# One more chunk of the first layer by seven products, and the weight sums held behind the splits

## The chip, the cores and the metric

The kernel runs on one core of a Trainium2 chip. The metric is the device time of one execution in microseconds, the median of the runs shown.

## What is computed

Pooled attention (keys and values averaged over 8 tokens, so 576 tokens see 72 pooled ones), and after it a two-layer network with a leaky ReLU, all of it in float32.

```python
B, H, S, D = 8, 8, 576, 64            # q is 8x, k is 8x the drawn values
k_p = k.reshape(B, H, 72, 8, D).mean(axis=3)
v_p = v.reshape(B, H, 72, 8, D).mean(axis=3)
scores = matmul(q, k_p.T) / 8;  attn = softmax(scores)
x = matmul(attn, v_p)                  # as 4608 rows of 512
h = x @ w_in                           # 512 -> 2048
out = maximum(0.01 * h, h) @ w_out     # 2048 -> 512
```

## The kernel before

**Chunks and runs.** The 4608 rows are worked as nine chunks of 512, numbered 0 to 8 (chunk 6 is the seventh). The network is most of the work. A float32 operand is split into a high and a low part (types fp32r), and a product of two such operands is three matmuls: high by high, high by low, low by high. The first layer of a chunk is 16 steps `f` of 128 hidden units; one step (`m1`, L1141 to L1143) is 12 matmuls of 512 columns into the PSUM tile `ph`. ScalarE (ACT) then applies the leaky ReLU in place (L1146) and makes the high part `gh` (L1149), VectorE (DVE) makes the low part `gl` (L1150). The second layer of a step (`m2`, L1327 to L1329) is again 12 matmuls of 512 columns, into four accumulators, and it trails `m1` by two steps. `ph` has two buffers, so `m1` of step f+2 can start only when `gl` of step f is done. `runs` lists the chunks in order: the first five entries share out chunks 0 and 1, after that each entry is one chunk, 2 to 8.

**Attention beside it.** The attention that fills chunk c+1 is done during the run of chunk c. TensorE (PE) makes the scores `pss` (L599), ACT the exponentials (L609), GpSimd (POOL) the normalized rows `at` (L643, L649). These go to DRAM and come back turned (`rows`, `blocks`, issued by SyncE, SP), DVE turns them (L680), ACT and DVE split them into `pT` (L702, L705), and PE multiplies by the pooled values (`pa`, L724 to L727). ACT and DVE write the result as the split tiles `xh`, `xl` of the next chunk.

**Keys and values.** `lk` and `lv` load and pool the keys and values of one batch: SP issues the loads of `k0raw`, `k1raw`, `kremraw`, `v0raw`, `v1raw`, `vremraw`, POOL adds them up (L264, L271) to `ksum`, `vsum`, `vremsum`. ACT scales `ksum` (L349), and later, when the batch's turn comes, `v_hi` (L512) and `v_parts` (L521) are made of the value sums. The raw tiles all come from the pool tag `raw`, which has two buffers.

**Seven products.** From chunk `FAST` on, the first layer goes by pairs of steps: a 2 by 2 block product in seven block products in place of eight (`pair`, `product`, L1233), each six matmuls of 256 columns, 42 to a pair, eight pairs to a chunk. It needs sums of weight blocks. `prepare(j)` makes them for pair j (DVE L1180 to L1186, ACT `wsumh` L1189, DVE L1190), in two tiles of the tag `raw`, and SP writes them to the DRAM tile `kept` (L1200). They come back for each pair through ACT's queue (`stream`, L1225). `combine` makes sums and splits of the x blocks (POOL L797, ACT, DVE L793). The eight pairs' weight sums are spread over four runs, chunks 2 to 5, two pairs each, in the first half of each run; `lk` and `lv` stand at the middle of a run's attention units.

**What sets the order.** PE's order is written out by hand. The other engines' orders are made by a scheduler, which fills each queue with what its own model of the time finds ready, so that an instruction can stand ahead of others that the program issued before it. From the first seven-product chunk on (`pinned`), POOL's and SP's orders are the program's too, and attention follows `line_up_pinned` in place of `line_up_via`. `tc.issue_after(ins)` holds back what is issued inside it until `ins` is in its queue. An engine works its queue strictly in order.

Of the kernel before, what the change touches and what calls it, by code (L numbers as in the profile page):

```python
# [24 lines left out]
def tile_pooled_attention_ffn(  # L25
# [44 lines left out]
    VIA = 2  # L70
    SPLIT = 8
    HALF = CH // 2
    FAST = 7


    PAIRS = [(4, 0), (5, 1), (6, 2), (7, 3), (8, 9), (10, 11), (12, 13), (14, 15)]
# [422 lines left out]
    def place_v(b, sums, rem):  # L499
        if b < 2:  # L500
            pvm = bank(b, f"pvm{b}").rearrange("a p x -> a (p x)")[:, : NK * D]
            for g, half in enumerate(sums):
                for i in range(2):
                    nc.tensor.matmul(
                        pvm[:, 2 * g * D : 2 * (g + 1) * D],
                        addup[:, 1 - i : 3 - i, :].rearrange("r i s -> r (i s)"),
                        half[:, i::2, :], start=i == 0, stop=i == 1,
                    )
            sums = pvm.rearrange("a (p d) -> a p d", p=NK)
        for i in range(2):  # L510
            r = slice(64 * i, 64 * i + 64)
            pin(nc.scalar.mul(v_hi[r, :, i, :], sums[r], 1.0 / POOL))  # L512
        for i in range(2):
            r = slice(64 * i, 64 * i + 64)
            pin(nc.vector.scalar_tensor_tensor(
                v_lo[r, :, i, :], sums[r], 1.0 / POOL, v_hi[r, :, i, :].bitcast(F32),
                op0=ALU.mult, op1=ALU.subtract,
            ))
        if b > 1:
            yield  # L520
            pin(nc.scalar.mul(v_parts, rem, 1.0 / POOL))  # L521
            yield
            pin(nc.vector.scalar_tensor_tensor(
                rem, rem, 1.0 / POOL, v_parts.bitcast(F32), op0=ALU.mult, op1=ALU.subtract
            ))
            nc.vector.tensor_scalar(rem, rem, signs[:, 1:2], None, op0=ALU.mult)
            nc.vector.scalar_tensor_tensor(
                rem, v_parts.bitcast(F32), signs[:, 0:1], rem, op0=ALU.mult, op1=ALU.add
            )
            nc.vector.tensor_tensor(  # L530
                v_rem, rem.unsqueeze(2).broadcast_to([P, 2, 4, D]),
                heads.unsqueeze(1).unsqueeze(3).broadcast_to([P, 2, 4, D]), op=ALU.mult,
            )
            return
        for g in range(2):
            r, lo = slice(32 * g, 32 * g + 32), slice(64 + 32 * g, 96 + 32 * g)
            nc.scalar.mul(v_parts[r, g], rem[r, 0], 1.0 / POOL)
            nc.vector.scalar_tensor_tensor(
                v_parts[lo, g], rem[r, 0], 1.0 / POOL, v_parts[r, g].bitcast(F32),
                op0=ALU.mult, op1=ALU.subtract,  # L540
            )
        pv = bank(b, f"pv{b}").rearrange("a p x -> a (p x)")[:, : 2 * D]
        nc.tensor.matmul(
            pv, spread, v_parts.rearrange("s g d -> s (g d)"), start=True, stop=True
        )
        nc.vector.tensor_tensor(
            v_rem, pv.rearrange("s (g d) -> s g d", g=2).unsqueeze(2).broadcast_to([P, 2, 4, D]),
            heads.unsqueeze(1).unsqueeze(3).broadcast_to([P, 2, 4, D]), op=ALU.mult,
        )
# [574 lines left out]
    parts = [(n, c, f) for n, (c, fs, _) in enumerate(runs) for f in fs]  # L1124
    partial = dram.tile([CH, DM], F32, name="partial")
    back = []
    gs, accs = {}, {}

    def m1(k):

        n, c, f = parts[k]
        xh, xl = x_parts(c)
        w = ws[0, f]
        ts = runs[n][2]
        r = slice(ts[0] * P, (ts[-1] + 1) * P)
        w_ = len(ts) * P
        nm = f"{n}_{f}"
        ph = ps_h.tile([P, CH], F32, tag="h", name=f"ph{nm}")[:, :w_]
        for kk in range(NK):
            ks = slice(kk * P, (kk + 1) * P)  # L1140
            nc.tensor.matmul(ph, w[:, 0, ks], xh[kk][:, r], start=kk == 0, stop=False)  # L1141
            nc.tensor.matmul(ph, w[:, 0, ks], xl[kk][:, r], start=False, stop=False)  # L1142
            nc.tensor.matmul(ph, w[:, 1, ks], xh[kk][:, r], start=False, stop=kk == NK - 1)  # L1143
            if kk == 1:
                yield
        nc.scalar.activation(ph, ph, AF.Prelu, alpha=0.01)  # L1146
        gh = three.tile([P, CH], F32R, tag="gh", name=f"gh{nm}")[:, :w_]
        gl = three.tile([P, CH], F32R, tag="gl", name=f"gl{nm}")[:, :w_]
        casts.append(nc.scalar.copy(gh, ph))  # L1149
        nc.vector.tensor_tensor(gl, ph, gh.bitcast(F32), op=ALU.subtract)  # L1150
        gs[k] = gh, gl
        yield

# [16 lines left out]
    def prepare(j):  # L1170

        f0, f1 = PAIRS[j]
        raw = two.tile([P, 2, DM], F32, tag="raw", name=f"wsum{j}")
        w = [raw[:, k, :] for k in range(2)]
        raw = two.tile([P, 2, DM], F32R, tag="raw", name=f"wsumh{j}")
        h = [raw[:, k, :] for k in range(2)]
        (a11, a12), (a21, a22) = ((x[:, :HALF], x[:, HALF:]) for x in w)
        for x, f in zip(w, (f0, f1)):
            whole = ws[0, f].bitcast(F32)
            nc.vector.tensor_tensor(x, whole[:, 0, :], whole[:, 1, :], op=ALU.add)  # L1180
            yield
        nc.vector.tensor_tensor(a22, a21, a22, op=ALU.add)
        nc.vector.tensor_tensor(a21, a11, a21, op=ALU.subtract)
        yield
        nc.vector.tensor_tensor(a11, a22, a11, op=ALU.subtract)
        nc.vector.tensor_tensor(a12, a12, a11, op=ALU.subtract)  # L1186
        yield
        for x, y in zip(w, h):
            nc.scalar.copy(y, x)  # L1189
            nc.vector.tensor_tensor(x.bitcast(F32R), x, y.bitcast(F32), op=ALU.subtract)  # L1190
            yield
        ship = [
            (kept[j, :, 2 - 2 * i : 4 - 2 * i, k, :], part.rearrange("p (s x) -> p s x", s=2))
            for i in range(2) for k, part in enumerate((h[i].bitcast(F32), w[i]))
        ]
        if j < OPEN:
            ship.append((kept[j, :, 4], ws[0, f1].bitcast(F32)[:, :, HALF:]))
        yield
        for to, of in ship:
            nc.sync.dma_start(to, of)  # L1200
        yield

    seats = {}
# [139 lines left out]
    def store(n, c, t, a):  # L1343
        end = n == len(runs) - 1
        if end and t == NT - 1:

            r = 2 * S - 2 * TAIL + (c - 2) * CH + t * P
            for i, copy in enumerate((nc.scalar.copy, nc.vector.tensor_copy)):
                cols = slice(i * DM // 2, (i + 1) * DM // 2)
                o = two.tile([P, DM // 2], F32, tag="raw", name=f"o{n}_{t}{i}")  # L1350
                copy(o, a[:, cols])
                (nc.scalar if i == 0 else nc.sync).dma_start(out[r : r + P, cols], o)
            return

        pool, tag = (two, "raw") if n == REST - 1 and t > 1 else (five, "o")
        o = pool.tile([P, DM], F32, tag=tag, name=f"o{n}_{t}")
        if end:
            if t % 2:
                nc.scalar.copy(o, a)
            else:  # L1360
                nc.vector.tensor_copy(o, a)
        elif n == REST:
            nc.vector.tensor_tensor(o, a, back[t], op=ALU.add)
        else:
            nc.scalar.copy(o[:, : DM // 2], a[:, : DM // 2])
            nc.vector.tensor_copy(o[:, DM // 2 :], a[:, DM // 2 :])
        if n == 0:
            nc.sync.dma_start(partial[t * P : (t + 1) * P, :], o)
        elif c < 2:
            nc.sync.dma_start(out[c * S + t * P : c * S + (t + 1) * P, :], o)  # L1370
        elif c == 2 and t == 0:
            for b in range(2):
                nc.sync.dma_start(out[b * S + CH : (b + 1) * S, :], o[TAIL * b : TAIL * (b + 1), :])
        else:
            r = 2 * S - 2 * TAIL + (c - 2) * CH + t * P
            nc.sync.dma_start(out[r : r + P, :], o)


    steps = []
# [99 lines left out]
        early[max(n, REST) - 1].append(b)  # L1479

    PIECES_OF = 8
    EACH = -(-len(PAIRS) // (FAST - 3))

    def sums_of(js):
        for j in js:
# [4 lines left out]
    for n, (c, fs, ts) in enumerate(runs[: REST + FAST - 1]):  # L1490
# [3 lines left out]
        if n >= REST:  # L1494
            nxt = n - REST + 2
            if nxt in waiting:
                us.insert(0, lambda nxt=nxt: carry(nxt))
            mid = len(us) // 2
            for b in early[n]:
                us[mid:mid] = [att[b]["lk"], att[b]["lv"]]  # L1500
            if n == REST:
# [5 lines left out]
        for f in fs:  # L1507
# [23 lines left out]
            for slot in slots:  # L1531
                for _ in slot:
                    beat += 1
                    while done < min(len(us), len(us) * beat // (beats - behind)):
                        us[done]()
                        done += 1
                    while n > REST and formed < min(1, 2 * beat / beats) * PIECES_OF * EACH:
                        formed += 1
                        next(forming, None)
            at += 1  # L1540
        while done < len(us):
            us[done]()
# [80 lines left out]
```

## Time and profile before

| | |
|---|---|
| median of 3 runs | 923.64 us (922.68, 923.64, 926.41) |
| profiled execution | 926.44 us, span 924.7 us |
| PE busy, share of span | 890.6 us, 96% |
| DVE, ACT, POOL busy | 499.3, 433.4, 211.2 us |
| granted TensorE clock, mean | 0.987 |
| chunk 2's run | 253.0 to 355.6 us |
| chunk 3's run | 355.6 to 450.5 us |
| chunk 4's run | 450.5 to 548.8 us |
| chunk 5's run | 548.8 to 645.3 us |
| chunk 6's run | 645.3 to 739.2 us |
| chunk 7's run (seven products) | 739.2 to 830.5 us |
| chunk 8's run (seven products, no attention beside it) | 830.5 us to the end |

A run is taken from the start of its chunk's first first-layer matmul to that of the next chunk's. PE's busy share counts pipelined matmuls and says little about how dense they are; the distance between the starts of two matmuls in the timeline does.

### The profile page before, as it was taken

The numbers are of one execution on the slowest core, as the hardware profiler recorded it, in microseconds if no ns is written. First come the engines' busy times: TensorE is split into PE (matmuls) and PEld (weight loads), VectorE is DVE, ScalarE is ACT, GpSimd is POOL, SyncE is SP. The second block draws the span as 40 slices with busy tenths as digits, with TensorE's granted clock in tenths as the row PEclk, the third lists the DMA queues.
The fourth block names the chain that finished last, engine by engine and source line by source line (L and its number), as shares of the span: only waits on it lengthen the run. The fifth ranks groups of instructions, "written<-read, shape, count | busy, mean of one in ns | idle before, by whom it ended". The sixth has DMA issues, their size and how long they took to land.

```text
span 924.7 us, 13658 instructions
## 1 busy us (share of the span) xinstructions
PE 890.6 (96%) x4587; PEld 761.1 (82%) x4587; DVE 499.3 (54%) x1178; ACT 433.4 (47%) x1354; POOL 211.2 (23%) x388
## 2 busy tenths in 40 slices
PE   4599999999999989999999999999999999999998
PEld 4478888788888868888888878888888889989997
DVE  6999569545384572636555555553455442452222
ACT  5788558344344443533444345342544344453332
POOL 4511110343423312411232122411210321010000
PEclk9799999999999989999999999999999999999999
DMA  9985231427346453423534343620532055414342
GB/s 259 303 262 166 66 72 46 97 58 188 111 130 171 107 162 86 113 47 120 154 82 96 87 137 102 138 62 25 148 81 63 0 164 160 122 47 137 105 135 80
DMA packets 153029, 108.37 MB, mean 117 GB/s; under 512 B 99840, under 2 KB 133376, under 8 KB 152960
## 3 DMA queue, kind: packets, MB, share of 16 engines
q1 hardware_dynamic: 144976, 90.86, 36.4%
q10 hardware_dynamic: 7984, 16.65, 6.4%
q8 instruction: 36, 0.59, 0.3%
q14 instruction: 33, 0.27, 0.1%
HBM read 76.94 MB, written 30.54 MB: 116 GB/s over the span
## 4 chain that ended last, share of the span: by engine, by line
PE 80%; DVE 7%; DMA 5%; POOL 2%; SPq 2%; ACT 2%; issue 1%; POOLq 0%; ACTq 0%; DVEq 0%
PE acc L1327 12%; PE acc L1328 12%; PE acc L1329 12%; PE ph L1141 9%; PE ph L1143 9%; PE ph L1142 9%; PE ends_y L1233 5%; PE ends_x L1233 3%; PE pss L599 3%; DMA q<-in_q_dram 1%; DMA blocks<-rows 1%; PE pa L725 1%; PE pa L727 1%; PE pa L726 1%; PE pa L724 1%
## 5 line engine op out<-in xcount | busy, mean ns | idle before, releaser
L1327 PE MATMUL acc<-w,gh 128*128 128x512 f32 x576 | 227.6, 395 | 0.0
L1328 PE MATMUL acc<-w,gh 128*128 128x512 f32 x576 | 225.2, 391 | 0.0
L1329 PE MATMUL acc<-w,gl 128*128 128x512 f32 x576 | 224.5, 390 | 0.0
L1141 PE MATMUL ph<-xh,w 128*128 128x512 f32 (+1 forms) x480 | 185.4, 386 | 3.6 <-DVE gl L1150 3.6
L1142 PE MATMUL ph<-xl,w 128*128 128x512 f32 (+1 forms) x480 | 181.9, 379 | 0.0
L1143 PE MATMUL ph<-xh,w 128*128 128x512 f32 (+1 forms) x480 | 181.9, 379 | 0.0
L1329 PEld LDWEIGHTS acc<-w,gl 128*128 128x128 f32 x576 | 108.2, 188 | 23.4
L1146 ACT ACTIVATE ph<-ph 128x512 f32<-128x512 f32 (+1 forms) x120 | 67.1, 559 | 127.0 <-PE ph L1143 126.3
L609 ACT ACTIVATE e<-pss,red 128x72 f32<-128x72 f32 (+1 forms) x320 | 97.6, 328 | 57.5 <-DVE red L607 57.2
L1327 PEld LDWEIGHTS acc<-w,gh 128*128 128x128 f32 x576 | 108.5, 188 | 19.2
L1328 PEld LDWEIGHTS acc<-w,gh 128*128 128x128 f32 x576 | 108.5, 188 | 18.6
L1150 DVE TENSOR_TENSOR gl<-ph,gh 128x512 fp32r<-128x512 f32 (+1 forms) x120 | 77.6, 648 | 74.7 <-ACT gh L1149 73.7
L1141 PEld LDWEIGHTS ph<-xh,w 128*128 128x128 f32 x480 | 91.5, 191 | 19.8 <-DVE gl L1150 4.2
L1143 PEld LDWEIGHTS ph<-xh,w 128*128 128x128 f32 x480 | 91.3, 190 | 16.9
L1142 PEld LDWEIGHTS ph<-xl,w 128*128 128x128 f32 x480 | 91.4, 190 | 15.4
L643 POOL TENSOR_TENSOR at<-e,red 128x128 f32<-128x128 f32 (+1 forms) x120 | 48.4, 423 | 193.1 <-DVE red L640 116.1
L1149 ACT CAST gh<-ph 128x512 fp32r<-128x512 f32 (+1 forms) x120 | 67.1, 559 | 3.1
L609 ACT ACTIVATION_READ_ACCUMULATOR e<-pss,red 128x1 f32 (+1 forms) x320 | 68.4, 214 | 0.0
L607 DVE TENSOR_REDUCE red<-pss 128x4 f32<-128x288 f32 (+1 forms) x80 | 35.9, 453 | 55.8 <-PE pss L599 53.1
L680 DVE STREAM_TRANSPOSE pp<-blocks 128x384 f32<-128x384 f32 (+1 forms) x60 | 44.4, 760 | 38.6 <-DMA blocks<-rows 38.5
L702 ACT CAST pT_hi<-pp 128x384 fp32r<-128x384 f32 (+1 forms) x80 | 36.4, 479 | 45.9 <-DVE pp L680 42.6
L599 PE MATMUL pss<-kT,qT 128*128 128x144 f32 x320 | 48.8, 294 | 3.8 <-DVE qT L564 1.1
(244 smaller groups left out, 1263.5 us busy)
## 6 DMA issues: line engine op xcount, KB each, us to landing
seat<-kept ACTq DMA_DIRECT2D x21, 512.0 KB
rows<-at SPq DMA_DIRECT2D x48, 192.0 KB
blocks<-rows SPq DMA_DIRECT2D x48, 192.0 KB
out_dram<-o SPq DMA_DIRECT2D x34, 256.0 KB
w_bits<-in_moe_w_in_dram SPq DMA_DIRECT2D x16, 512.0 KB
w_bits<-in_moe_w_out_dram SPq DMA_DIRECT2D x16, 512.0 KB
q<-in_q_dram SPq DMA_DIRECT2D x96, 64.0 KB
kept<-wsumh SPq DMA_DIRECT2D x16, 256.0 KB
```

The costliest lines, as they stand in the source:

```text
L599: nc.tensor.matmul(sc[:, 2 * SP * i : 2 * SP * (i + 1)], qT[:, p, :], kT[:, p, :, :].rearrange("d i s -> d (i s)"), start=True, stop=True,)
L609: ins = nc.scalar.activation(e[:n, h, :], scv[:n, h, :], AF.Exp, bias=mx[:n, h : h + 1], accum_out=sm[:n, h : h + 1],)
L1141: nc.tensor.matmul(ph, w[:, 0, ks], xh[kk][:, r], start=kk == 0, stop=False)
L1142: nc.tensor.matmul(ph, w[:, 0, ks], xl[kk][:, r], start=False, stop=False)
L1143: nc.tensor.matmul(ph, w[:, 1, ks], xh[kk][:, r], start=False, stop=kk == NK - 1)
L1146: nc.scalar.activation(ph, ph, AF.Prelu, alpha=0.01)
L1149: casts.append(nc.scalar.copy(gh, ph))
L1150: nc.vector.tensor_tensor(gl, ph, gh.bitcast(F32), op=ALU.subtract)
L1233: nc.tensor.matmul(out, w[:, stay, ks], move, start=start and i + n == 0, stop=i + n == 3, skip_group_check=True,)
L1327: nc.tensor.matmul(a, gh[:, r], hi, start=first, stop=False)
L1328: nc.tensor.matmul(a, gh[:, r], lo, start=False, stop=False)
L1329: nc.tensor.matmul(a, gl[:, r], hi, start=False, stop=last)
```

## The change

Chunk 6 is now worked with seven products, with all that hangs on it (its attention results go unsplit to `x_next`, its attention beside follows the pinned order, POOL and SP are pinned one run earlier). The weight sums still stand in four runs, chunks 2 to 5, two pairs each, but from beat 8 to beat 30 of a run's 64 (a beat is half an `m1` or half an `m2`), and each piece is held back until the last `gh` and `gl` issued so far are in their queues. `lk` and `lv` stand at two thirds of a run's attention units. `v_parts` is held back behind `v_hi`. The copy of a resident weight half to `kept` is held back behind the last store of the output.

```diff
-    FAST = 7
+    FAST = 6
...
-            pin(nc.scalar.mul(v_hi[r, :, i, :], sums[r], 1.0 / POOL))
+            ins = pin(nc.scalar.mul(v_hi[r, :, i, :], sums[r], 1.0 / POOL))
...
-            pin(nc.scalar.mul(v_parts, rem, 1.0 / POOL))
+            with tc.issue_after(ins.ins):
+                pin(nc.scalar.mul(v_parts, rem, 1.0 / POOL))
...
-        nc.vector.tensor_tensor(gl, ph, gh.bitcast(F32), op=ALU.subtract)
+        lows.append(nc.vector.tensor_tensor(gl, ph, gh.bitcast(F32), op=ALU.subtract))
...
-        if j < OPEN:
-            ship.append((kept[j, :, 4], ws[0, f1].bitcast(F32)[:, :, HALF:]))
         yield
         for to, of in ship:
             nc.sync.dma_start(to, of)
+        if j < OPEN:
+            with tc.issue_after(sent[-1].ins):
+                nc.sync.dma_start(kept[j, :, 4], ws[0, f1].bitcast(F32)[:, :, HALF:])
...
-            nc.sync.dma_start(out[r : r + P, :], o)
+            sent.append(nc.sync.dma_start(out[r : r + P, :], o))
...
-    EACH = -(-len(PAIRS) // (FAST - 3))
+    EACH = -(-len(PAIRS) // (FAST - 2))
+    FROM, UNTIL = 8, 30
...
-            mid = len(us) // 2
+            mid = len(us) * 2 // 3 if n > REST else len(us) // 2
             for b in early[n]:
                 us[mid:mid] = [att[b]["lk"], att[b]["lv"]]
...
-                    while n > REST and formed < min(1, 2 * beat / beats) * PIECES_OF * EACH:
+                    while n > REST and formed < min(1, (beat - FROM) / (UNTIL - FROM)) * PIECES_OF * EACH:
                         formed += 1
-                        next(forming, None)
+                        with tc.issue_after(casts[-1].ins), tc.issue_after(lows[-1].ins):
+                            next(forming, None)
```

In the rows below a name's first digits are its batch, tile or step: `ph5_11` is step 11 of chunk 2 (the sixth entry of `runs`, counted from 0), `ph6_9` step 9 of chunk 3, `wsumh2` the high part for the third pair, `o9_0` the first output tile of chunk 6, `o8_0` that of chunk 5.

ACT's queue in the second half of chunk 2's run, before:

```order
L609 ACTIVATE e3_2_0_3469,red3_2_0_3470<-pss3_2_0_3466,red3_2_0_3470 64x72 x4
L609 ACTIVATE e3_2_1_3479,red3_2_1_3480<-pss3_2_1_3476,red3_2_1_3480 64x72 x4
L1189 CAST wsumh2_3741<-wsum2_3740 128x512 x2
L521 ACTIVATE v_parts_107<-vremsum4_3296 128x128
L1146 ACTIVATE ph5_11_3506<-ph5_11_3506 128x512
L702 CAST pT_hi_118<-pp3_0_0_3553 128x3x128
L1149 CAST gh5_11_3520<-ph5_11_3506 128x512
```

and in the changed kernel:

```order
L610 ACTIVATE e3_2_0_3469,red3_2_0_3470<-pss3_2_0_3466,red3_2_0_3470 64x72 x4
L610 ACTIVATE e3_2_1_3479,red3_2_1_3480<-pss3_2_1_3476,red3_2_1_3480 64x72 x4
L1147 ACTIVATE ph5_11_3506<-ph5_11_3506 128x512
L703 CAST pT_hi_118<-pp3_0_0_3553 128x3x128
L1150 CAST gh5_11_3520<-ph5_11_3506 128x512
```

The third pair's `wsumh` and the next batch's `v_parts` stood ahead of step 11's ReLU; now neither does. The third pair's casts now stand in chunk 3's run, behind `gh6_3`, and that batch's `v_parts` behind its `v_hi`.

ACT's queue where `ksum` of batch 5 is scaled, in chunk 3's run, before:

```order
L1146 ACTIVATE ph6_3_3927<-ph6_3_3927 128x512
L349 ACTIVATE ksum5_4170<-ksum5_4170 128x256
L1149 CAST gh6_3_3948<-ph6_3_3927 128x512
L1146 ACTIVATE ph6_4_3977<-ph6_4_3977 128x512
L1149 CAST gh6_4_4002<-ph6_4_3977 128x512
```

and in the changed kernel:

```order
L703 CAST pT_hi_118<-pp3_4_1_4244 128x3x128
L1147 ACTIVATE ph6_8_4217<-ph6_8_4217 128x512
L1150 CAST gh6_8_4238<-ph6_8_4217 128x512
L349 ACTIVATE ksum5_4313<-ksum5_4313 128x256
L610 ACTIVATE e4_1_0_4264,red4_1_0_4265<-pss4_1_0_4261,red4_1_0_4265 128x72 x4
L610 ACTIVATE e4_1_1_4274,red4_1_1_4275<-pss4_1_1_4271,red4_1_1_4275 128x72 x4
L1147 ACTIVATE ph6_9_4281<-ph6_9_4281 128x512
L1150 CAST gh6_9_4303<-ph6_9_4281 128x512
```

The scaling moved from step 3 to behind step 8, nine rows and two steps behind the last `wsumh` of the run (not shown), whose buffers the key loads take over; two groups of exponentials and step 9's ReLU stand behind it.

DVE's queue at the start of the first seven-product run, before (chunk 7):

```order
L1366 COPY o9_0_7558<-acc9_0_6725 128x256
L1366 COPY o9_1_7565<-acc9_1_6729 128x256
L1264 TENSOR_TENSOR gl10_0_7546<-dia10_0_7468,gh10_0_7545 128x512
L1366 COPY o9_2_7595<-acc9_2_6741 128x256
L1264 TENSOR_TENSOR gl10_0_7589<-off10_0_7467,gh10_0_7588 128x512
L1366 COPY o9_3_7604<-acc9_3_6745 128x256
L564 STREAM_TRANSPOSE qT7_3_7624<-q7_3_6936 128x4x128
```

and in the changed kernel (chunk 6):

```order
L1369 COPY o8_0_6677<-acc8_0_5763 128x256
L565 STREAM_TRANSPOSE qT6_3_6681<-q6_3_5986 128x4x128
L1266 TENSOR_TENSOR gl9_0_6669<-dia9_0_6580,gh9_0_6668 128x512
L1369 COPY o8_1_6686<-acc8_1_5767 128x256
L608 TENSOR_REDUCE red6_3_0_6718<-pss6_3_0_6714 128x4
L608 TENSOR_REDUCE red6_3_1_6728<-pss6_3_1_6724 128x4
L1266 TENSOR_TENSOR gl9_0_6711<-off9_0_6579,gh9_0_6710 128x512
L640 TENSOR_TENSOR red6_3_0_6718<-red6_3_0_6718,tiny_120 128x4
L641 RECIPROCAL red6_3_0_6718<-red6_3_0_6718 128x4
L565 STREAM_TRANSPOSE qT6_4_6787<-q6_4_6654 128x2x4x32
L1369 COPY o8_2_6737<-acc8_2_5781 128x256
```

The turned queries of the second attention tile stood behind all four output copies and stand now behind one; those of the third stand ahead of the third and fourth.

## Rows read from the trace of the kernel before

**Rows 1.** The page: busy time of each engine, and the chain that ended last by engine.
```profile
PE 890.6 (96%) x4587; PEld 761.1 (82%) x4587; DVE 499.3 (54%) x1178; ACT 433.4 (47%) x1354; POOL 211.2 (23%) x388
...
PE 80%; DVE 7%; DMA 5%; POOL 2%; SPq 2%; ACT 2%; issue 1%; POOLq 0%; ACTq 0%; DVEq 0%
```

**Rows 2.** Stretches, chunks 2 to 8: length, busy (count) by engine, clock, DMA share, GB/s.
```profile
253.00:355.60 102.60, 99.39 (x458) 83.14 (x458) 62.94 (x151) 43.31 (x143) 31.90 (x55) 0.97 0.51 136
355.60:450.50 94.90, 94.90 (x449) 79.80 (x448) 50.27 (x118) 38.85 (x124) 20.08 (x40) 1.00 0.38 101
450.50:548.80 98.30, 96.72 (x457) 81.27 (x456) 55.89 (x139) 43.00 (x146) 26.40 (x51) 1.00 0.41 107
548.80:645.30 96.50, 96.50 (x458) 81.28 (x457) 47.45 (x119) 40.00 (x138) 26.27 (x51) 1.00 0.35 86
645.30:739.20 93.90, 93.90 (x447) 79.15 (x445) 46.85 (x113) 43.12 (x143) 19.27 (x39) 1.00 0.27 72
739.20:830.50 91.30, 90.22 (x569) 81.49 (x568) 38.98 (x81) 42.23 (x125) 13.37 (x23) 1.00 0.43 125
```

**Rows 3.** Timeline of PE, chunk 2's run: start, length, what, idle before and its releaser.
```profile
331.36 0.79 PE L1141 MATMUL ph<-xh,w 128*128 128x512 f32 x1 [3.21 <-DVE gl L1150]
```

**Rows 4.** Timeline of ACT, the same place.
```profile
327.51 1.14 ACT L1189 CAST wsumh<-wsum 128x512 fp32r<-128x512 f32 x2 [7.34 <-POOL vremsum L271]
328.56 0.30 ACT L521 ACTIVATE v_parts<-vremsum 128x128 fp32r<-128x128 f32 x1
328.77 0.57 ACT L1146 ACTIVATE ph<-ph 128x512 f32<-128x512 f32 x1
```

**Rows 5.** Stretch behind that stall: columns as in rows 2.
```profile
331.00:337.00 6.00, 5.64 (x14) 4.49 (x15) 5.28 (x13) 1.83 (x4) 0.00 (x0) 0.50 0.79 254
```

**Rows 6.** Timeline, chunk 4's run: ACT, then PE.
```profile
533.26 1.15 ACT L1189 CAST wsumh<-wsum 128x512 fp32r<-128x512 f32 x2 [8.64 <-POOL vremsum L271]
...
539.68 0.39 PE L725 MATMUL pa<-pT_lo,v_hi 128*128 128x256 f32 x1 [1.58 <-DVE pT_lo L705]
```

**Rows 7.** Timeline of PE, one `m1` of 12 matmuls: its first, and what follows its last.
```profile
322.55 0.39 PE L1141 MATMUL ph<-xh,w 128*128 128x512 f32 x1
...
325.26 0.39 PE L1327 MATMUL acc<-w,gh 128*128 128x512 f32 x1
```

**Rows 8.** Chain in order of time: two block products (12 matmuls) of chunk 7.
```profile
739.36 1.43 PE ends_x L1233 x12
```

**Rows 9.** Groups by line, chunk 7: weight loads of a block product, count | busy, mean ns.
```profile
L1233 PEld LDWEIGHTS ends_x<-T17xh,seat 128*128 128x128 f32 x32 | 5.6, 192 | 0.0
```

**Rows 10.** Timeline, chunk 7's run: ACT, DVE, PE around its one stall.
```profile
754.35 0.37 ACT L1365 COPY o<-acc 128x256 f32<-128x256 f32 x1 [1.33 <-DMA out_dram<-o]
...
754.76 0.42 DVE L1366 COPY o<-acc 128x256 f32<-128x256 f32 x1 [2.85 <-ACT o L1365]
755.10 1.07 DVE L564 STREAM_TRANSPOSE qT<-q 128x512 f32<-128x512 f32 x1
...
756.23 1.00 PE L599 MATMUL pss<-kT,qT 128*128 128x144 f32 x6 [1.08 <-DVE qT L564]
```

**Rows 11.** Groups by line and shape: ReLU, high part, low part of a step.
```profile
L1146 ACT ACTIVATE ph<-ph 128x512 f32<-128x512 f32 x104 | 61.0, 587 | 122.6 <-PE ph L1143 121.9
...
L1149 ACT CAST gh<-ph 128x512 fp32r<-128x512 f32 x104 | 61.1, 588 | 2.7
...
L1150 DVE TENSOR_TENSOR gl<-ph,gh 128x512 fp32r<-128x512 f32 x104 | 70.9, 683 | 71.4 <-ACT gh L1149 70.5
```

**Rows 12.** Timeline, chunk 2's run: key loads on SP, `ksum` on ACT.
```profile
288.02 1.32 SPq L287 DMA_DIRECT2D k0raw<-in_k_dram  x2
...
298.27 0.42 ACT L349 ACTIVATE ksum<-ksum 128x256 f32<-128x256 f32 x1 [6.10 <-POOL ksum L271]
298.59 0.58 ACT L1146 ACTIVATE ph<-ph 128x512 f32<-128x512 f32 x1
```

**Rows 13.** Timeline of POOL, end of chunk 6's run: the last x sum of `combine`.
```profile
728.61 1.74 POOL L797 TENSOR_TENSOR x<-x,x 128x512 f32<-128x512 f32 x1
```

More of the change, by code (lines that the diff above doesn't have):

```diff
@@ L1126, in tile_pooled_attention_ffn @@
     back = []
-    gs, accs = {}, {}
+    gs, accs, lows, sent = {}, {}, [], []
     def m1(k):
@@ L1353, in store @@
             return
-        pool, tag = (two, "raw") if n == REST - 1 and t > 1 else (five, "o")
+        apart = n == REST - 1 and t > 1
+        pool, tag = (two, "raw") if apart else (five, "o")
         o = pool.tile([P, DM], F32, tag=tag, name=f"o{n}_{t}")
@@ L1369, in store @@
         elif c < 2:
-            nc.sync.dma_start(out[c * S + t * P : c * S + (t + 1) * P, :], o)
+            sent.append(nc.sync.dma_start(out[c * S + t * P : c * S + (t + 1) * P, :], o))
         elif c == 2 and t == 0:
```

## The prediction

> **What bounds the kernel.** I read the page first, then the stretches chunk by chunk, then PE's timeline wherever a stretch is longer than its work, and last what released the engine that PE waited for. The page names PE: it is busy for 96% of the span, and 80% of the chain that ended last is PE [rows 1]. So time is won in two ways only, by giving PE less to stream or by closing holes in its stream. The stretches show where the holes are: chunks 3, 5 and 6 have PE busy from end to end, chunk 2 lacks 3.2 us, chunk 4 1.6 us and chunk 7 1.1 us [rows 2]. Chunks 2 and 5 have the same 458 matmuls in them, yet chunk 2 takes 102.6 us and chunk 5 96.5.
>
> **The hole in chunk 2.** PE idles 3.21 us before an `m1` and is released by `gl` [rows 3]. `gl` is late because ACT stood still for 7.34 us, until POOL's `vremsum` let go of the buffer into which the cast `wsumh` writes [rows 4]; the ReLU of the step came only after it, at 328.77. That cast belongs to the third pair, whose sums the program issues in chunk 3's run; the scheduler had drawn it forward. Behind the hole the granted clock is 0.50, the 1.2 GHz level, from 331 to 337 us with PE busy [rows 5]; before it PE had run at 2.4 GHz without a gap. So chunk 2's excess over chunk 5 is the idle time, 3.2 us, and some 2.9 us of half clock. Chunk 4 has the same cast, waiting 8.64 us for the same releaser, and PE then idles 1.58 us for `pT` [rows 6]; the clock stays up.
>
> **The change, part by part.**
>
> *Sums behind the splits, `v_parts` behind `v_hi`, key loads later.* ACT's queue shows both waiting instructions gone from ahead of step 11's ReLU, and the third pair's casts back in chunk 3, between two steps. Their buffers come there from value loads of the run before, long pooled. The work is the same, 16 casts and their DVE steps, only moved, and it stays beside PE's stream. I take the two holes as gone whole: 102.6 - 96.5 = **-6.1 us** for chunk 2 and 98.3 - 96.5 = **-1.8 us** for chunk 4 [rows 2]. Bounds: nothing, if another wait takes their place, and these sums, since chunk 5 has no hole to give.
>
> *Seven products in chunk 6.* Removed are 16 `m1`. One is 325.26 - 322.55 = 2.71 us from first start to the next matmul behind it [rows 7], so 16 are 43.4 us. Added are 8 pairs of 7 block products; two of these take 1.43 us [rows 8], so 56 take 40.0 us. The difference is **-3.3 us**. The second layer and the attention's matmuls stay as they are. The trace bounds it well, because chunk 7 already runs this way.
>
> What speaks against a finer cut is the weight load: 336 loads of 128 columns in place of 192. A load of a block product lasts 192 ns [rows 9], yet twelve matmuls with their twelve loads pass in 1.43 us [rows 8], so the loads lie under the matmuls before them. The Trainium skill, in "TensorE: Matmul & The Clock Gate", Part 3 (what overlaps and what doesn't), says that a weight load overlaps with matmuls in flight only where it goes to other row groups, and these go to all rows; by that the 144 more loads would stand in PE's way, and the sum would be that of the last rival below. The trace does not agree.
>
> *What the seven products bring with them, at no cost on PE.* Weight sums come back through ACT's queue for chunk 6 too: chunk 7 has a DMA share of 0.43 against chunk 6's 0.27 [rows 2], so both loads together come to no more than 0.70, under the 0.79 that the trace shows for a short while [rows 5]. `combine` now ends chunk 5, where attention, key loads and weight sums also lie. Its last POOL step ended at 730.4 us, 8.9 us before the 739.2 at which chunk 7 began [rows 13]. In the new order POOL has the next batch's value sums just ahead of it; if these come 9 us later than before, the start of chunk 6 waits. In rows 2 POOL is busy 26 of 96 us in chunk 5, so I take zero.
>
> *The start of the pinned run.* Chunk 7's one hole is at its start: an output tile waits for a store, DVE's copy waits for ACT's, the turned queries stand behind it, and PE waits 1.08 us for the scores' operand [rows 10]. The same start now comes at chunk 6 and again at chunk 7. The new queue has the second tile's queries behind one output copy in place of four, which speaks for less; five attention tiles beside chunk 6 in place of three speak for more. I price chunk 6's start as the row has it, **+1.1 us**, and leave chunk 7's as it was. Bounds: -1.1 (both gone) and +3.
>
> *The key scaling.* The loads now begin only when the run's second pair of sums has been written out, and the scaling of `ksum` on ACT stands two or three steps behind that pair's last cast, with exponentials and a ReLU queued behind it. From the first key load to the scaling took 298.27 - 288.02 = 10.3 us [rows 12]; two steps of `m1` and `m2` are 4 x 2.71 = 10.8 us. So ACT comes to the scaling at about the moment it can go, or a few us early, since the sums must first land. The slack is: `gl` of a step is wanted when two `m2` and one `m1` have passed, 3 x 2.71 = 8.1 us, less ReLU, `gh` and `gl`, 0.59 + 0.59 + 0.68 [rows 11], which leaves 6.3 us. A wait of 6.10 us on this very scaling cost PE nothing [rows 12], one of 7.34 us cost 3.2 [rows 4]. I take zero; the bounds are 0 and 6.1 us a chunk (3.2 idle and 2.9 of half clock, as in chunk 2).
>
> **The sum.** -6.1 - 1.8 - 3.3 + 1.1 = -10.1 us, against the profiled execution's own 926.44 us (924.7 of span and 1.7 around it): **916.3 us**. That execution is 2.8 us above the median of 923.64; two of the runs shown lie near 923 and one near 926.4. The gap is about what the half clock cost, but no row tells whether the others had it, and a kernel without the hole has neither, so I forecast from the profiled one. Against the median it is -7.3 us, 0.8%. A measurement of this kernel can tell about 0.5% from no change, 4.6 us: faster is under 919.0, slower over 928.3.
>
> **The rivals.**
>
> 1. *The wait comes back at the key scaling, in one of the four runs* (chunks 2 to 5). For it: key loads moved behind the sums, and 4 us of exponentials queue behind the scaling. Against it: 6.10 us cost nothing. 916.3 + 6.1 = 922.4 us. Chance 0.14.
> 2. *The same in three or four of the runs*, since all four have the same order. It decides where ACT's wait passes some 6 us of slack on every run, that is where the key loads land 4 to 6 us later than I reckon. Four times 6.1: 916.3 + 24.4 = 940.7 us, slower than before. Chance 0.06.
> 3. *Attention beside the pinned chunk 6 holds PE up.* Five tiles in place of three, with POOL's and SP's order fixed, or `combine` late at the end of chunk 5. At chunk 7's hole for each tile, five times 1.1, in place of one: 916.3 + 4.4 = 920.7 us. For it: the order was followed with three tiles only. Against it: DVE, ACT and POOL are under half busy there [rows 2]. Chance 0.10.
> 4. *The holes stay*: the cast is held at the tail of another wait and chunks 2 and 4 lose what they lost. 916.3 + 7.9 = 924.2 us. Against it the queue's order, plainly. Chance 0.04.
> 5. *Weight loads stand in the way*: 144 more loads at 192 ns [rows 9] are 27.6 us in place of the 3.3 won: 947 us. Chunk 7's 91.3 us, with 336 such matmuls, rules it out. Chance 0.01.
>
> That leaves 0.65 for the forecast: holes gone, seven products at their streamed cost, a stray hole of a microsecond or two.
>
> **How the numbers follow.** The likeliest case gives 916.3. Its own range is 912.5 (both pinned starts clean, and small gaps closed) to 919.0. To hold 8 in 10 the range must reach rival 3 and the first chunk of rival 1: 912.5 to 922.5; left out are rivals 2, 4 and 5 and the far side of 1. Faster by over 0.5%: 0.65 for the forecast, less 0.03 for its upper edge, and 0.13 from the milder half of rivals 1 and 3 (a hole without half clock, 3.2 us, ends near 919), 0.75. Slower: rivals 2 and 5, 0.07. Within: the rest, 0.18.
>
> **What would show it.** Right: chunk 2 at 96 to 97 us and chunk 4 at 96.5 with PE busy throughout; no wait of `wsumh` or `v_parts` for `vremsum`; the clock at 1.00 from chunk 2 to the end; chunk 5 about 2.7 us shorter than before and chunk 6 near 94.4, because four second-layer tiles pass from the one to the other, 12 matmuls at 0.226 us (chunk 6's stretch has 447 matmuls where its neighbours have up to 458 [rows 2]). Wrong: ACT waiting over 6 us for `ksum` with PE idle for `gl` behind it (rivals 1 and 2); holes before the scores or `pT` in chunk 6 (rival 3); 56 block products over 42 us (rival 5).

## The result, and the profile after

| | before | after |
|---|---|---|
| median | 924.44 us (922.68 to 926.41, 4 runs) | 938.40 us (937.79 to 939.08, 4 runs) |
| ratio, 95% interval | | 1.0150 (1.0132 to 1.0168) |
| profiled execution, span | 926.44, 924.7 us | 938.04, 936.2 us |
| mean granted clock | 0.987 | 0.984 |

The change costs 1.5%. The lengths of chunks here and below are each of one profiled execution, and executions of one kernel differ by 1 to 5 us; the medians and their intervals decide. The stretches of the kernel after, chunks 2 to 7, with the columns of [rows 2]:

```profile
253.00:357.00 104.00, 98.95 (x458) 82.39 (x457) 55.55 (x131) 40.29 (x138) 28.50 (x51) 0.98 0.42 109
357.00:459.50 102.50, 97.70 (x450) 81.45 (x449) 49.74 (x118) 38.85 (x124) 25.60 (x44) 0.97 0.38 103
459.50:555.90 96.40, 96.40 (x457) 81.23 (x456) 55.83 (x135) 42.59 (x142) 29.69 (x51) 1.00 0.42 111
555.90:655.90 100.00, 96.42 (x447) 80.30 (x446) 59.22 (x131) 44.72 (x147) 33.35 (x56) 0.98 0.44 118
655.90:753.20 97.30, 96.19 (x610) 86.54 (x610) 59.97 (x140) 52.84 (x183) 21.48 (x42) 1.00 0.55 144
753.20:842.10 88.90, 88.90 (x561) 80.43 (x560) 39.26 (x77) 40.73 (x113) 13.47 (x23) 1.00 0.43 129
```

Against [rows 2], chunk 4 is 1.9 us shorter and chunk 7 2.4: chunk 4's hole is gone, and so is the one at chunk 7's start. Chunk 2 is 1.4 us longer, chunk 3 7.6, chunks 5 and 6 together 6.9. Chunk 3 had been dense from end to end; now PE lacks 4.8 us of its stretch.

In chunk 3 the chain is read backwards, from PE's timeline (start, length, what, idle before and its releaser):

```profile
430.53 0.79 PE L1142 MATMUL ph<-xh,w 128*128 128x512 f32 x1 [4.80 <-DVE gl L1151]
```

`gl` is late because ACT stands. ACT's timeline of the same place:

```profile
413.92 0.42 ACT L349 ACTIVATE ksum<-ksum 128x256 f32<-128x256 f32 x1 [8.05 <-POOL ksum L271]
414.24 0.30 ACT L610 ACTIVATE e<-pss,red 128x72 f32<-128x72 f32 x1
...
426.32 0.51 ACT L703 CAST pT_hi<-pp 128x384 fp32r<-128x384 f32 x1 [5.86 <-DVE pp L681]
428.61 0.51 ACT L703 CAST pT_hi<-pp 128x384 fp32r<-128x384 f32 x1 [1.78 <-DVE pp L681]
429.03 0.58 ACT L1147 ACTIVATE ph<-ph 128x512 f32<-128x512 f32 x1
```

Two casts of `pT` stand in its queue ahead of the ReLU and wait for DVE's turned tile `pp`, which waits for the attention rows coming back from DRAM (DVE's timeline):

```profile
425.43 0.86 DVE L681 STREAM_TRANSPOSE pp<-blocks 128x384 f32<-128x384 f32 x1 [6.85 <-DMA blocks<-rows]
```

Those transfers were issued late. SP's timeline of chunk 3 in the kernel before, the loads and the last tiles' transfers:

```profile
343.22 1.33 SPq L287 DMA_DIRECT2D k0raw<-in_k_dram  x2
...
381.17 1.33 SPq L287 DMA_DIRECT2D v0raw<-in_v_dram  x2
...
415.29 0.45 SPq L669 DMA_DIRECT2D blocks<-rows  x1
...
417.11 4.07 SPq L669 DMA_DIRECT2D blocks<-rows  x3
```

and in the kernel after, with the stores of the weight sums ahead of the loads:

```profile
381.10 0.38 SPq L1199 DMA_DIRECT2D kept<-wsumh  x1
...
401.99 0.36 SPq L1199 DMA_DIRECT2D kept<-wsum  x1
403.82 1.35 SPq L287 DMA_DIRECT2D k0raw<-in_k_dram  x2
...
413.91 1.27 SPq L287 DMA_DIRECT2D v0raw<-in_v_dram  x2
...
422.56 0.51 SPq L670 DMA_DIRECT2D blocks<-rows  x1
...
425.10 2.02 SPq L670 DMA_DIRECT2D blocks<-rows  x3
```

The key loads start 60.6 us later, the value loads 32.7, the `blocks` transfers 7.3 and 8.0 (the chunk itself begins 1.4 us later). Two things lie in between. One is the key scaling: the exponentials stand in ACT's queue behind it and start at 414.24, though DVE had their row maxima ready at 408.90:

```profile
407.95 0.95 DVE L608 TENSOR_REDUCE red<-pss 128x4 f32<-128x288 f32 x2 [1.35 <-PE pss L600]
```

The other is POOL, where the sums of the late loads lie in front of the attention's products `at`, whose reciprocals were ready at 415.95 and 417.16. `at` begins 4.1 us behind the first of them; in the kernel before it began at 413.02, 0.13 us behind:

```profile
415.97 1.29 POOL L264 TENSOR_TENSOR kremraw<-kremraw 64x256 f32<-64x256 f32 x2 [2.09 <-DMA kremraw<-in_k_dram]
...
418.80 1.29 POOL L264 TENSOR_TENSOR v0raw<-v0raw 128x512 f32<-128x512 f32 x1 [0.19 <-DMA v0raw<-in_v_dram]
420.05 0.76 POOL L644 TENSOR_TENSOR at<-e,red 128x128 f32<-128x128 f32 x2
```

After the idle time the clock is for the most part at the 1.2 GHz level. A stretch of the kernel after:

```profile
432.00:436.00 4.00, 4.00 (x12) 3.14 (x11) 3.70 (x9) 0.09 (x1) 0.55 (x1) 0.55 0.17 49
```

In chunks 2 and 5 the end of the chain is the same, and another piece of the late loads is seen in it: the eight remainder loads of the values. Chunk 2 has a hole of 2.11 us at 330.41, and two more, of 2.03 and 0.91 us, from 335.45 on. The first comes through SP, in whose queue the eight loads stand ahead of a transfer of `blocks`:

```profile
316.87 5.40 SPq L317 DMA_DIRECT2D vremraw<-in_v_dram  x8
...
324.40 0.62 SPq L670 DMA_DIRECT2D blocks<-rows  x1
```

The others come through POOL, where the sum of these loads stands ahead of the last tile's `at`, whose first reciprocals were ready at 317.06:

```profile
325.97 1.29 POOL L264 TENSOR_TENSOR vremraw<-vremraw 128x512 f32<-128x512 f32 x1 [6.55 <-DMA q<-in_q_dram]
327.22 0.75 POOL L644 TENSOR_TENSOR at<-e,red 64x128 f32<-64x128 f32 x2
```

In chunk 5 it is SP's queue again:

```profile
625.51 5.41 SPq L317 DMA_DIRECT2D vremraw<-in_v_dram  x8
630.96 0.45 SPq L670 DMA_DIRECT2D blocks<-rows  x1
```

### The profile page after: what moved, and what is told of

It is laid out like the page before. It is cut to its first block, busy times and chain, and to the rows that moved or that the text cites. A ratio compares the mean times of both kernels' runs of the same rounds, so it can differ in the third digit from the quotient of the medians.

```text
span 936.2 us, 14043 instructions
## 1 busy us (share of the span) xinstructions
PE 893.4 (95%) x4731; PEld 767.0 (82%) x4731; DVE 515.4 (55%) x1189; ACT 443.4 (47%) x1381; POOL 225.9 (24%) x394
## 4 chain that ended last, share of the span: by engine, by line
PE 48%; DMA 8%; DVE 4%; POOL 3%; SPq 3%; ACT 2%; issue 1%; ACTq 0%; DVEq 0%; POOLq 0%
PE acc L1329 8%; PE acc L1330 8%; PE acc L1331 8%; PE ends_y L1235 7%; PE ends_x L1235 5%; PE ph L1142 3%; PE ph L1143 3%; PE ph L1144 3%; DMA blocks<-rows 3%; PE pss L600 2%; DMA kept<-wsumh 1%; SPq L317 1%; DMA k1raw<-in_k_dram 1%; DVE pp L681 1%; POOL at L644 1%
## 5 line engine op out<-in xcount | busy, mean ns | idle before, releaser
L1142 PE MATMUL ph<-xh,w 128*128 128x512 f32 (+1 forms) x416 | 160.2, 385 | 7.3 <-DVE gl L1151 7.3
L1143 PE MATMUL ph<-xl,w 128*128 128x512 f32 (+1 forms) x416 | 157.0, 377 | 0.0
L1144 PE MATMUL ph<-xh,w 128*128 128x512 f32 (+1 forms) x416 | 156.7, 377 | 0.0
L1147 ACT ACTIVATE ph<-ph 128x512 f32<-128x512 f32 (+1 forms) x104 | 57.8, 555 | 111.2 <-PE ph L1144 110.7
L644 POOL TENSOR_TENSOR at<-e,red 128x128 f32<-128x128 f32 (+1 forms) x120 | 54.4, 472 | 201.6 <-DVE red L641 100.9
L1151 DVE TENSOR_TENSOR gl<-ph,gh 128x512 fp32r<-128x512 f32 (+1 forms) x104 | 66.9, 643 | 64.2 <-ACT gh L1150 63.5
L1142 PEld LDWEIGHTS ph<-xh,w 128*128 128x128 f32 x416 | 79.4, 191 | 21.8 <-DVE gl L1151 8.3
L1144 PEld LDWEIGHTS ph<-xh,w 128*128 128x128 f32 x416 | 79.2, 190 | 14.4
L1143 PEld LDWEIGHTS ph<-xl,w 128*128 128x128 f32 x416 | 79.3, 191 | 13.2
L1150 ACT CAST gh<-ph 128x512 fp32r<-128x512 f32 (+1 forms) x104 | 57.8, 556 | 2.7
```

The costliest lines, as they stand in the source:

```text
L644: nc.gpsimd.tensor_tensor(at[:n, :, i, :].rearrange("a (h f) j -> a h f j", h=2), e[:n, 2 * i : 2 * i + 2, 0:MAIN].rearrange("a h (f j) -> ...
L1151: lows.append(nc.vector.tensor_tensor(gl, ph, gh.bitcast(F32), op=ALU.subtract))
```

## The experiments

The change has three parts that could do this: the later place of the loads (theory A), the sums' place and hold (rival B), the seven products of chunk 6 (rival C). The first four runs take each alone, or take one away.

**The loads back at the middle of a run.**

```diff
-            mid = len(us) * 2 // 3 if n > REST else len(us) // 2
+            mid = len(us) // 2
```

> The changed kernel with the k and v loads of the runs after chunk 1's put back to the middle of a run; sums behind the splits and seven products from chunk 6 stay. Theory A (the later loads are what costs: they put the raw loads of v, eight of them for the remainders at 5.4 us of SP, directly ahead of the last attention tiles' transfers in SP's queue, and the pT casts that wait for these hold ReLU and gh): 916 to 922 us, and chunks 3 and 5 without the pT holes. Rival B (the sums, formed later in a run and queued behind splits, take the raw buffers later and so delay the loads): 932 to 940 us. Rival C (the seven-product chunk 6 and its x sums): 932 to 940 us.

Measured: 939.04 us, ratio to before 1.0158 (1.0133 to 1.0183). The first key load of chunk 3 is at 406.00 us, no earlier than with the loads at two thirds. So theory A falls in this, that the loads' place in the program makes them late; that late loads do harm is not touched by it.

**The later loads alone, on the kernel before** (the same line the other way).

> The kernel before with one line of the change: k and v loads at two thirds of a run. Theory A: 930 to 942 us, with pT holes of 3 to 8 us in chunks 2, 3 and 5. Rivals B and C: 922 to 927 us, as before.

Measured: 926.45 us, 1.0028 (1.0016 to 1.0041). The first key load of chunk 3 is at 342.36, within a microsecond of where it was. The place of the loads in the program costs 0.3% and does not make them late.

**The sums behind the splits alone, on the kernel before.**

```diff
-        nc.vector.tensor_tensor(gl, ph, gh.bitcast(F32), op=ALU.subtract)
+        lows.append(nc.vector.tensor_tensor(gl, ph, gh.bitcast(F32), op=ALU.subtract))
...
+    FROM, UNTIL = 8, 30
...
-                    while n > REST and formed < min(1, 2 * beat / beats) * PIECES_OF * EACH:
+                    while n > REST and formed < min(1, (beat - FROM) / (UNTIL - FROM)) * PIECES_OF * EACH:
                         formed += 1
-                        next(forming, None)
+                        with tc.issue_after(casts[-1].ins), tc.issue_after(lows[-1].ins):
+                            next(forming, None)
```

> The kernel before with the sums alone queued behind the splits, in the middle third of a run; loads at the middle and seven products from chunk 7 as before. Theory A: the ACT holes of chunks 2 and 4 go, 916 to 922 us. Rival B: 930 to 942 us. Rival C: 916 to 925 us.

Measured: 935.78 us, 1.0125 (1.0097 to 1.0153), chunk 3 102.8 us, and its first key load as late as in the changed kernel:

```profile
404.63 1.35 SPq L287 DMA_DIRECT2D k0raw<-in_k_dram  x2
```

That is most of the whole loss, so rival B holds.

**Seven products from chunk 6 alone, on the kernel before.**

```diff
-    FAST = 7
+    FAST = 6
...
-    EACH = -(-len(PAIRS) // (FAST - 3))
+    EACH = -(-len(PAIRS) // (FAST - 2))
```

> The kernel before with the seven products alone, from chunk 6, and the sums over the same four runs by the rule of before. Theory A: 920 to 924 us (3.3 us from seven products, about 1 back at the chunk's start, the holes of before stay). Rival B: 920 to 924 us too. Rival C: 930 to 942 us.

Measured: 923.75 us, 0.9991 (0.9976 to 1.0007): no difference that can be told. Rival C falls. Chunks 5 to 7 take 280.4 us together in place of 281.7.

With this a new theory, D. All raw tiles share two buffers and take turns in program order. In the kernel before, the scheduler let the sums of a run go ahead to the end of the run before, and the key loads behind them came 12 us before their run began. Held to the splits of their own run, the sums keep both buffers until its middle, and all loads of the run wait.

**The hold taken away, the rest of the change kept** (`next(forming, None)` without the two `issue_after`).

> The changed kernel with the sums no longer queued behind the splits; their place in the program (beats 8 to 30), the later loads and the seven products from chunk 6 stay. Theory D (the hold keeps the sums, and with them the two raw buffers, until the middle of a run, so the k and v loads that follow in the same two buffers start some 55 us later than before; what is late then is the last attention tiles): the sums go ahead to the end of the run before again, the key loads of chunk 3 start near 343 us in place of 404, and the time is 920 to 926 us with the old wsumh holes back. Rival E (the place of the sums in the program is what costs, held or not): 932 to 940 us.

Measured: 925.93 us, 1.0024 (1.0013 to 1.0035). The first key load of chunk 3 comes as theory D has it; chunks 3 and 5 are back at 95.1 and 94.0 us, chunk 2 at 103.2.

```profile
345.26 1.32 SPq L287 DMA_DIRECT2D k0raw<-in_k_dram  x2
```

**The hold kept, the sums placed earlier.**

```diff
-    FROM, UNTIL = 8, 30
+    FROM, UNTIL = 0, 12
```

> The changed kernel with the sums still queued behind the splits, but placed in beats 0 to 12 of a run in place of 8 to 30. Theory D: the buffers come free some 25 us earlier, key loads of chunk 3 near 375 to 385 us, and half or more of the loss goes: 920 to 930 us. Rival F (holding the sums by the splits costs wherever they stand, through DVE's and ACT's order): 934 to 940 us.

Measured: 923.59 us, 1.0000 (0.9987 to 1.0014). Chunk 2 falls to 98.1 us, so the hold by itself does not cost the 1.5% (rival F falls). Chunk 5 still takes 99.2, 5.2 more than with the sums free, with PE idle 2.55 us for `pT` in it. The first key load of chunk 3:

```profile
372.41 1.37 SPq L287 DMA_DIRECT2D k0raw<-in_k_dram  x2
```

**The loads held, the sums free, on the kernel before.** ACT writes one column into each key buffer behind the middle split, so that the load must wait (the list `held` is filled only while `lk` is worked in chunks 2 to 5).

```diff
+        if nm == "k" and held:
+            with tc.issue_after(casts[-1].ins):
+                nc.scalar.copy(raw[:, 0, 0:1], ident[:, 0:1])
```

> The kernel before, its sums free as they were, with only the key loads held: a copy of one column by ACT, queued behind the split at the middle of a run, writes into each key buffer ahead of its load. Theory D: late loads alone do the harm, key loads of chunk 3 near 400 us, PE holes for pT or gl late in chunks 3 to 5, and 930 to 942 us. Rival G (late sums do the harm and late loads don't): 922 to 927 us.

Measured: 937.78 us, 1.0154 (1.0135 to 1.0173). SP's timeline of chunk 3 has the sums stored early and the loads late:

```profile
345.11 0.45 SPq L1205 DMA_DIRECT2D kept<-wsum  x1
...
396.73 1.36 SPq L292 DMA_DIRECT2D k0raw<-in_k_dram  x2
```

Chunks 3 to 5 take 98.9, 101.6 and 98.4 us against 94.9, 98.3 and 96.5 of [rows 2]. So late loads are enough to cost as much as the change does, and rival G falls. That the totals agree is in part luck, for the paths differ: in chunks 3 and 4 of this run a good part is free sums that wait for the late remainder loads and hold ACT. ACT's timeline of chunk 3:

```profile
436.02 1.15 ACT L1194 CAST wsumh<-wsum 128x512 fp32r<-128x512 f32 x2 [7.41 <-POOL vremsum L271]
```

No run has the sums late and the loads early; that late sums do no harm but through the loads is argued, not shown.

**The casts and rests of the sums by POOL** (`nc.gpsimd` in place of ACT and DVE, with `FAST = 6`, on the kernel before).

> The kernel before with seven products from chunk 6, and the cast and the rest of each weight sum computed by POOL in place of ACT and DVE; nothing held. POOL is the engine that frees the buffers, so no other engine's queue waits for vremsum. Theory D: loads as early as before, the ACT holes of chunks 2 and 4 gone: 914 to 920 us. Rival H (POOL gets late with the attention's products): 922 to 930 us.

Measured: 925.73 us, 1.0020 (1.0006 to 1.0034); a miss. Chunk 4 does come to 96.4 us, but chunk 2 takes 105.4: with `wsumh` gone from ACT's queue, the next instruction waits for the same releaser. ACT's timeline of this run, and behind it DVE's and POOL's:

```profile
328.35 0.31 ACT L521 ACTIVATE v_parts<-vremsum 128x128 fp32r<-128x128 f32 x1 [6.73 <-POOL vremsum L271]
...
330.11 3.04 DVE L527 SCALAR_TENSOR_TENSOR vremsum<-v_parts,signs,vremsum 128x128 f32<-128x128 f32 x1
...
330.52 2.47 POOL L1190 TENSOR_TENSOR wsum<-wsum,wsumh 128x512 fp32r<-128x512 f32 x2
```

PE's hole there is 6.02 us, against 3.21 in [rows 3]. The difference comes from DVE: its step L527, 0.33 us in the kernel before, takes 3.04 us and ends with POOL's two rests beside it, and `gl` stands behind it.

**The remainder loads through POOL's queue, on the changed kernel.**

```diff
-                    nc.sync.dma_start(
+                    nc.gpsimd.dma_start(
                         raw[32 * h : 32 * h + 32, g, :],
```

> The changed kernel with the eight remainder loads of v sent out by POOL's queue in place of SP's, nothing else. Theory D1 (the late loads harm by standing in SP's queue ahead of the last tiles' transfers; the eight take 5.4 us there): the blocks transfers of chunks 2 and 5 go out 4 to 5 us earlier, their pT holes shrink, and the time is 926 to 933 us. Theory D2 (the late loads harm by their data, through POOL's pooling that comes late and holds at, or through v_rem): 935 to 942 us.

Measured: 929.49 us, 1.0053 (1.0032 to 1.0073). Chunk 2 falls from 104.0 to 99.4 us and chunk 5 from 100.0 to 97.8; chunk 3 stays at 101.4, with PE idle 4.56 us for `gl`, as there the remainder loads were issued behind the tiles' transfers. So D1 is right for chunk 5, and D2 for chunk 3, where the key scaling and POOL's order hold `at`. In chunk 2 both moved: the transfers went out earlier, and `at` (323.65) now stands ahead of the sum of the remainder loads (326.21).

**The hold in chunk 3's run alone**, beats 0 to 12, loads at the middle.

```diff
+    UNTIL, HELD = 12, (REST + 2,)
...
+            mid = len(us) // 2
...
+                    held = n in HELD
+                    share = beat / UNTIL if held else 2 * beat / beats
...
+                        if not held:
+                            next(forming, None)
+                            continue
```

> The changed kernel with the loads at the middle again and the sums held by the splits only in chunk 3's run, in its first 12 beats; in the other runs they are free and in the first half, as in the kernel before. Theory D: chunk 2 keeps the 98 us and chunk 3 the 95.7 us of the run with early held sums, chunks 4 and 5 the 97.3 and 93.9 us of the run with free sums; against the 924.9 us span of that free run it is 5 us less: 918 to 922 us. Rival: chunk 2's hole comes back with the loads at the middle: 922 to 926 us.

Measured: 924.85 us, 1.0014 (1.0004 to 1.0024); a miss. Chunks 3 to 5 came as expected (95.6, 97.2, 93.9 us), chunk 2 did not (103.0). No cast waits for `vremsum` there any more, and yet the chunk is as long as before.

**The same with the last run's sums by POOL.**

> As the run with the hold in chunk 3's run only, and the last run's sums (the two pairs formed for chunk 5's run) cast and subtracted by POOL, so that ACT has no wsumh cast to wait with at the end of chunk 4. Theory D: chunk 4 at 96.5 in place of 97.3 us, the rest the same: 917 to 921 us. Rival H (POOL late with at): chunk 5 longer by 2 us, 920 to 924 us.

Measured: 924.65 us, 1.0010 (0.9999 to 1.0021); a miss. Chunk 4 is clean at 96.4 us, chunk 2 again 103.0. What is left there is seen in the timelines of ACT, SP and POOL:

```profile
333.55 0.76 ACT L703 CAST pT_hi<-pp 128x384 fp32r<-128x384 f32 x2 [6.06 <-DVE pp L681]
...
314.62 5.38 SPq L317 DMA_DIRECT2D vremraw<-in_v_dram  x8
...
322.12 0.62 SPq L670 DMA_DIRECT2D blocks<-rows  x1
327.75 0.63 SPq L661 DMA_DIRECT2D rows<-at  x1
...
330.01 4.33 SPq L670 DMA_DIRECT2D blocks<-rows  x5
...
324.31 2.12 POOL L264 TENSOR_TENSOR vremraw<-vremraw 128x512 f32<-128x512 f32 x2 [9.60 <-DMA q<-in_q_dram]
326.39 0.75 POOL L644 TENSOR_TENSOR at<-e,red 64x128 f32<-64x128 f32 x2
```

The casts wait for the `blocks` issued at 330.01, these for the `rows` of the last tile, and these for its `at`. SP stands idle from 322.74 to 327.75, so its queue is not what holds them. POOL's is: the sum of the eight remainder loads waits 9.60 us for them (the profile names `q`, which counts on the same semaphores), and `at`, whose first reciprocals were ready at 317.18, stands behind that sum.

**All three together:** that kernel with the remainder loads through POOL's queue.

> The run with the hold in chunk 3's run only and the last sums by POOL, and its eight remainder loads of v sent out by POOL's queue. Theory D1: in chunk 2 these eight stood in SP's queue right ahead of the last tile's q loads and blocks transfers, with pT holes of 3.0 and 1.1 us and 1.7 us of half clock behind them; the transfers go out 4 to 5 us earlier, most of that goes, and the time is 917 to 921 us, the fastest here. Rival: issuing holds POOL for 4.7 us in all four runs, at comes late with it, and the time is 923 to 928 us.

Measured: **918.12 us, 0.9939 (0.9926 to 0.9953)**, the fastest kernel here. Its stretches, chunks 2 to 5:

```profile
252.60:349.00 96.40, 96.40 (x457) 81.24 (x456) 58.68 (x137) 40.76 (x138) 33.10 (x59) 1.00 0.45 117
349.00:444.40 95.40, 95.25 (x449) 79.75 (x448) 55.47 (x128) 40.91 (x128) 30.57 (x55) 1.00 0.51 141
444.40:540.90 96.50, 96.50 (x458) 81.29 (x457) 56.03 (x131) 40.63 (x138) 37.11 (x65) 1.00 0.38 99
540.90:634.80 93.90, 93.90 (x447) 79.08 (x446) 46.45 (x115) 42.46 (x143) 35.20 (x64) 1.00 0.41 104
```

Chunk 2 goes from 103.0 to 96.4 us by where eight loads are issued. POOL's queue has another order with it, `at` ahead of the sum, and the last `blocks` go out at 323.02 in place of 330.01:

```profile
313.56 5.11 POOL L317 DMA_DIRECT2D vremraw<-in_v_dram  x8
318.69 0.77 POOL L644 TENSOR_TENSOR at<-e,red 64x128 f32<-64x128 f32 x2
...
322.29 2.31 POOL L264 TENSOR_TENSOR vremraw<-vremraw 128x512 f32<-128x512 f32 x2 [1.42 <-DMA vremraw<-in_v_dram]
```

No run changes POOL's order and leaves the loads to SP; that the order is what won the 6.6 us is read from the two traces. The Trainium skill, in "Perfetto Trace Analysis", section "DMA Optimizations", says that balancing DMAs over the engines that can issue them may help where an issuing engine looks busy with them. The gain here is not of that kind, as SP stood idle for 5.0 us just ahead of the late transfers before the move.

## Why the prediction was wrong

The forecast was 916.3 us, with 912.5 to 922.5 as its range; the kernel took 938.40 and became slower, not faster.

*The step that failed* is "Sums behind the splits, `v_parts` behind `v_hi`, key loads later", with its "only moved, and it stays beside PE's stream. I take the two holes as gone whole". The sums did move off ACT's critical place, as the queue showed. But while they wait they hold the two raw buffers, and with them every load of the run. The prediction saw that the loads "now begin only when the run's second pair of sums has been written out", followed them to the scaling of `ksum` and no further, and took zero; the value loads and their sums in POOL's and SP's queues had no price. The price was 1.25% with the hold alone and 1.54% with the loads alone held back. The runs with the hold away, with the sums early, and with the loads alone held back show it from three sides.

*The key scaling* was only the first link. Its wait came, 8.05 us in chunk 3, over the slack of 6.3, and PE went on for 11 us behind it, so right there it cost nothing, as taken. But the exponentials queued behind it came late with it, and then `at` behind POOL's sums, and at the end of that chain PE idled 4.80 us. Rival 2's 940.7 us is close to what was measured by luck: its mechanism was another one (PE was to idle for `gl` right behind the scaling), and in chunk 4 no hole came at all.

*-6.1 for chunk 2* was wrong in a second way. Its hole had two causes, one behind the other: the cast `wsumh`, and POOL's order, with the sum of the remainder loads ahead of the last tile's `at`. [Rows 4] name only the one that came last. Taking it away left 103.0 us; taking both left 96.4, which is the length that the step had reckoned from chunk 5.

*-1.8 for chunk 4* was right: 96.4 us.

*-3.3 and +1.1 for chunk 6.* The 56 block products (336 matmuls) are near their streamed cost: from start to start they take 40.7 us in the run with seven products alone, against 40.0 reckoned. So the 144 weight loads more cost next to nothing, and the line of the Trainium skill in "TensorE: Matmul & The Clock Gate", Part 3 (what overlaps and what doesn't), by which a weight load overlaps only where it goes to other row groups, does not agree with this trace. Chunk 6 took 97.5 us in that run where 94.4 was reckoned, and chunk 7 89.0 in place of 91.3, so chunks 5 to 7 gave 1.3 us in all and not 2.2. Some 1.2 us of both differences is work that changed its chunk: eight score matmuls more in chunk 6 and eight fewer in chunk 7, which the step had left where they were. Groups of the run with seven products alone (count | busy, mean ns | idle), chunk 6, then chunk 7; before, the two chunks had 40 (5.7 us busy) and 24 (3.5):

```profile
L599 PE MATMUL pss<-kT,qT 128*128 128x144 f32 x48 | 6.9, 287 | 0.2 <-DVE qT L564 0.2
...
L599 PE MATMUL pss<-kT,qT 128*128 128x144 f32 x16 | 2.3, 286 | 0.0
```

Chunk 7's start is clean, which gives the other 1.1 us there. Chunk 6 idles 1.1 us in all, as priced, but not at its start (the longest wait is 0.68 us for `pT` at 724.27); what remains of its 3.1 us is spread over short delays.

*By chunks*, against the lengths that the prediction implies (96.5, 94.9, 96.5, 93.8, 94.4, 91.3): +7.5, +7.6, -0.1, +6.2, +2.9, -2.4 us. The sum is 21.7, and 938.04 - 916.3 is 21.7.

## What to carry to other kernels

Before an instruction is held back, list what it holds while it waits: buffers of a shared ring, and every later taker of that ring, count as moved with it. The scheduler's running ahead looked like the fault here (a cast in the wrong place), and it was also what brought the loads in on time. A hole's releaser is the last of its causes, so a price of "gone whole" wants a look at what would be late next, in the order of every queue that the chain passes.

## What had not been expected of the hardware

Eight loads of one kind cost 5.4 us of SP's queue and 4.7 to 5.1 of POOL's, nearly the same. A DVE step of 0.33 us took 3.04 us beside two POOL steps of one tensor against another, and ended as they did. A hole of 4.80 us was followed by the 1.2 GHz level with PE busy, as in [rows 5]; in the run with the sums by POOL a hole of 2.13 us in chunk 5 was not, with the clock at 1.00 in the stretch behind it.
